# Retention and a GELU MLP on one core: seven-product groups in the first layer of blocks 3 to 6

## The chip, the cores and the metric

One core of a Trainium2 chip runs the whole program. The metric is the device time of one launch in microseconds (us). The engines are named as in the profile: PE is TensorE's matmul (PEld its weight load), DVE VectorE, ACT ScalarE, POOL GpSimd, SP SyncE, which here only issues transfers. Each engine works through its own instructions in order; a wait of one instruction holds up everything behind it on that engine.

## The reference

```python
# q, k, v: (8, 8, 576, 64) float32; w_in (512, 2048), w_out (2048, 512)
scores = matmul(q, k.T) / sqrt(64)
gamma = 1.0 - 2.0 ** (-5.0 - arange(8))                  # one decay for each head
Dmat = where(i >= j, gamma[:, None, None] ** (i - j), 0) # for positions i, j
x = matmul(scores * Dmat, v)                             # attention without softmax
x = x.transpose(0, 2, 1, 3).reshape(8 * 576, 512)        # 4608 tokens
h = x @ w_in
g = 0.5 * h * (1 + tanh(sqrt(2 / pi) * (h + 0.044715 * h ** 3)))
out = g @ w_out                                          # (4608, 512) float32
```

## The kernel before, in words

**Blocks.** The 4608 tokens are worked in nine blocks of 512 (`t` = 0 to 8, `NTB` = 9). Block `t` below 8 holds the first 512 positions of batch `t`; block 8 holds the last 64 positions of all eight batches (the tails, attended in pairs of batches: `TP`). While TensorE does the two MLP layers of block `t`, the attention of batch `t + 1` is done in between, the casts and transposes of batch `t + 2`, and the loads after that.

**A block has 30 steps.** Steps 0 to 15 are layer one, steps 16 to 29 layer two. `at(t, u, f)` hangs a piece of work behind step `u` of block `t`; `run` issues it there. So the order on each engine is written out by hand. Layer one (`up`, L474) takes the 16 column blocks of `w_in` one by one: four matmuls of 512 columns into a bank of PSUM ("a four" below), and a GELU on ScalarE into `gT`. Layer two (`prod`, L648) is done in all blocks by seven products in place of eight (Strassen and Winograd's form): VectorE makes sums of quarters of the activations (`act_sums`, L634: s1, s2, the difference in place, then s4), sums of quarters of `w_out` are made once (`weight_sums`, L623), and VectorE and ScalarE put the products together (`after`, L672), in the buffers k1, k2, k3.

**Seven products in layer one.** Blocks 7 and 8 (`WIN`) do three of four column groups of layer one in the same way. A group is 256 columns of the lower and 256 of the upper half of `w_in`, that is four column blocks. `in_sums` (L518) makes its sums of weights (during layer two of block 6), `x_sums` (L535) four sums of quarters of `xT` at the end of the block before. `up_prod` (L554) does one product: four matmuls of 256 columns. Products 1, 6, 7 and 4 of a group add up in one bank, B, so between them that bank is copied out: by ScalarE behind product 1 (into s) and behind 6 (into v), by VectorE behind 7 (into u). VectorE adds banks A and C to these copies, and ScalarE's GELU reads the results. A token such as "06" of the order `W_ORDER` means group 0, product 6; an empty one is a four.

**Attention.** For each batch four chunks of 128 positions: `score` (L379) and `masks` (L389, VectorE), `past` and `av` (L436, L455), `state` (L402) and on VectorE `scan` (L416: vs and ws, a running state with decay), which `spread` (L430) casts on ScalarE to a block-diagonal tile for `past`; `put` (L466) copies the result into `xT` on ScalarE. `later(b, c)` is scan and spread of a chunk.

**PSUM** has eight banks, handed out in the order in which they were given back (`bank`, `drop`). A bank is written again only when its last reader is done.

**Loads.** `seq` lists the loads of 256 KB in order; each takes one of sixteen buffers of the tag "ld" and gives it back when it is cast (`pump`, L141). A hold stops the list until `resume` at step 29. GpSimd casts keys and queries of batch `b` from step 16 of block `b - 2`, ScalarE the values. A copy of one element (`gate`, L978) lets GpSimd start its casts only when the last activation sum of the block has been made. All loads, the transposes (`turn_dma`, L305) and the outputs are issued on SP in one order.

## Time and profile before

| | |
|---|---|
| runs | 293.66 us median of 3 (293.11 to 294.78) |
| span of the profiled execution | 291.2 us |
| block 3, from its first matmul of layer one | 114.48 to 144.93 us |
| block 4 | 144.93 to 175.38 us |
| block 5 | 175.38 to 205.15 us |
| block 6 | 205.15 to 235.35 us |
| block 7 | 235.35 to 261.32 us |
| share of TensorE in the chain that ended last | 81% |
| loads of 256 KB, issue to landing, median | 5.2 to 5.9 us |

In the profile's lines a tile is written as output<-inputs, the number behind "x" counts instructions, and what stands in square brackets is how long the engine was idle before the instruction, and who released it. The windows give, for a stretch of time, its length and then the busy time of each engine in it.

### The profile page before, as it was taken

What the parts mean: (1) busy time and instruction counts of PE and PEld (TensorE: products, weight loads), DVE (VectorE), ACT (ScalarE), POOL (GpSimd) and SP (SyncE); (2) the same over time, 40 slices, a digit from 0 to 9 for tenths busy, and PEclk for the clock granted to TensorE, in tenths of its full rate; (3) what the DMA queues carried; (4) which work ended last, traced back from release to release, by engine and by line L of the source; (5) the groups of instructions that cost most, each with busy time, mean ns of one, the idle gap of its engine ahead of it and who ended that gap; (6) DMA issues with size and microseconds to landing.
All of it is one profiled execution on the core that took longest, in us unless ns stands there. A gap on an engine that the chain in (4) does not pass through costs nothing.

```text
span 291.2 us, 7390 instructions
## 1 busy us (share of the span) xinstructions
PE 280.6 (96%) x3028; PEld 208.4 (72%) x3028; DVE 204.2 (70%) x409; ACT 169.2 (58%) x320; POOL 100.5 (35%) x129
## 2 busy tenths in 40 slices
PE   6989998999999999999999999999999999999993
PEld 2568886888874687468845884488548887887783
DVE  5797998656864875477548834774489968974863
ACT  5278755896249545965396547664666258507810
POOL 4588869910760085008500740058030000000000
PEclk9999999999999999999999999999999999999999
DMA  7999999999989999999898979999951030003013
GB/s 196 308 367 360 379 294 240 245 235 179 224 168 243 227 204 194 254 229 199 169 234 204 229 155 239 224 202 157 265 106 38 2 144 3 0 24 122 3 36 108
DMA packets 139585, 53.95 MB, mean 185 GB/s; under 512 B 118048, under 2 KB 131360, under 8 KB 139552
## 3 DMA queue, kind: packets, MB, share of 16 engines
q1 hardware_dynamic: 138960, 52.97, 81.4%
q8 instruction: 23, 0.38, 0.5%
q10 hardware_dynamic: 592, 0.52, 0.5%
q14 instruction: 10, 0.08, 0.1%
HBM read 36.70 MB, written 9.44 MB: 158 GB/s over the span
## 4 chain that ended last, share of the span: by engine, by line
PE 81%; DMA 6%; POOL 5%; SPq 4%; DVE 1%; ACT 1%; issue 1%; POOLq 0%
PE hp L480 26%; PE opB L665 13%; PE opA L665 10%; PE opC L665 8%; PE hp L501 5%; DMA ld<-in_moe_w_in_dram 4%; PE hB L574 3%; SPq L96 3%; PE xs L459 3%; PE st L383 3%; POOL w_out_sb L771 2%; DMA ld<-in_q_dram 2%; PE hC L574 2%; PE xs L450 2%; PE opD L665 1%; PE us L408 1%
## 5 line engine op out<-in xcount | busy, mean ns | idle before, releaser
L480 PE MATMUL hp<-xT,w_in_sb 128*128 128x512 f16 x352 | 79.0, 379 | 0.0
L486 ACT ACTIVATE gT<-hp 128x512 f16<-128x512 f32 x88 | 50.1, 600 | 20.7 <-PE hp L480 20.1
L480 PEld LDWEIGHTS <-w_in_sb 128*128 128x128 f16 x352 | 34.0, 98 | 38.2
L665 PEld LDWEIGHTS <-gT 128*128 128x128 f16 x576 | 54.8, 98 | 8.9 <-issue 0.8
L665 PEld LDWEIGHTS <-s 128*128 128x128 f16 x432 | 42.1, 98 | 5.0
L642 DVE TENSOR_TENSOR s<-gT 128x512 f16<-128x512 f16 x36 | 15.6, 434 | 29.8 <-ACT gT L486 23.5
L665 PE MATMUL opA<-w_out_sb,gT 128*128 128x256 f16 x288 | 36.0, 273 | 0.4 <-ACT w_out_sb L771 0.3
L392 DVE TENSOR_TENSOR ret<-st,cm 128x512 f16<-128x512 f32 x48 | 30.1, 680 | 3.6 <-PE st L383 3.6
L469 ACT CAST xT<-xs 128x512 f16<-128x512 f32 x36 | 19.2, 591 | 18.7 <-PE xs L459 15.6
L501 PE MATMUL hp<-xT,w_in_sb 128*128 128x256 f16 x256 | 29.0, 273 | 0.0
L434 ACT CAST tbd<-ws 64x256 f16<-64x256 f32 x48 | 19.3, 403 | 15.3 <-DVE ws L425 14.7
L275 POOL TENSOR_TENSOR ck<-ld,sc 128x512 f16<-128x512 f32 x24 | 25.0, 1040 | 7.7 <-DMA ld<-in_k_dram 7.7
L978 POOL COPY gate<-s 128x1 f16<-128x1 f16 x5 | 0.9, 188 | 76.5 <-DVE s L646 76.5
L275 POOL TENSOR_TENSOR cq<-ld,sc 128x512 f16<-128x512 f32 x24 | 26.2, 1090 | 2.1 <-DMA ld<-in_q_dram 1.8
L501 PEld LDWEIGHTS <-w_in_sb 128*128 128x128 f16 x256 | 24.6, 98 | 3.1
L665 PE MATMUL opB<-wt,gT 128*128 128x256 f16 x224 | 26.8, 273 | 0.0
L262 ACT CAST cv<-ld 128x512 f16<-128x512 f32 x23 | 13.7, 618 | 18.9 <-DMA ld<-in_v_dram 18.8
L508 ACT ACTIVATE gT<-hp 128x512 f16<-128x512 f32 x32 | 18.3, 602 | 3.2 <-PE hp L501 3.0
L679 DVE TENSOR_TENSOR k<-k,opB 128x512 f32<-128x512 f32 x17 | 11.6, 685 | 12.0 <-PE opB L665 11.0
L425 DVE TENSOR_TENSOR ws<-vs,gt 128x256 f32<-128x256 f32 x24 | 18.2, 760 | 1.1
L665 PE MATMUL opB<-wt,s 128*128 128x256 f16 x144 | 17.4, 273 | 0.0
L665 PE MATMUL opC<-wt,s 128*128 128x256 f16 x144 | 17.2, 273 | 0.0
(122 smaller groups left out, 409.1 us busy)
## 6 DMA issues: line engine op xcount, KB each, us to landing
ld<-in_q_dram SPq DMA_DIRECT2D x32, 256.0 KB, 5.3
ld<-in_k_dram SPq DMA_DIRECT2D x32, 256.0 KB, 5.2
ld<-in_v_dram SPq DMA_DIRECT2D x32, 256.0 KB, 5.5
out_dram<-ost SPq DMA_DIRECT2D x16, 512.0 KB, 3.8
ld<-in_moe_w_in_dram SPq DMA_DIRECT2D x16, 256.0 KB, 5.9
ld<-in_moe_w_out_dram SPq DMA_DIRECT2D x16, 256.0 KB, 5.8
lt<-in_k_dram SPq DMA_DIRECT2D x8, 128.0 KB, 4.7
lt<-in_q_dram SPq DMA_DIRECT2D x8, 128.0 KB, 4.3
```

Source lines behind the costliest of these rows:

```text
L275: eng.tensor_tensor(out=dst.rearrange("p (h d) -> p h d", d=D), in0=raw.rearrange("p (h d) -> p h d", d=D), in1=sc[:, s0].unsqueeze(2).to_ ...
L392: nc.vector.tensor_tensor(out=r.rearrange("p (n i) -> p n i", i=128), in0=t.rearrange("p (n i) -> p n i", i=128), in1=(cm if b < PAIR else ...
L425: nc.vector.tensor_tensor(out=w, in0=uc, in1=gt, op=ALU.mult)
L434: cp(out=(tbd[b % 2][r, c, :, r] if c < NC - 1 else tbt[b % NT4][r, :, r]), in_=w[r])
L469: nc.scalar.copy(out=xT[:, g0 : g0 + 2], in_=xs.rearrange("p (n g t) -> p g n t", n=HP, g=2))
L480: nc.tensor.matmul(hp.rearrange("p (g t) -> p g t", t=TL), w_in_sb[:, ct, 128 * fc : 128 * fc + 128], xT[:, o : o + TB // TL, ct, :], star ...
L486: nc.scalar.activation(out=gT[t][:, fc].rearrange("p i n -> p (i n)"), in_=hp, func=AF.Gelu_apprx_tanh)
L501: nc.tensor.matmul(hps[n][:, 256 * x : 256 * x + 256].rearrange("p (g t) -> p g t", t=TL), w_in_sb[:, ct, 128 * (fs[n] + x) : 128 * (fs[n] ...
L508: nc.scalar.activation(out=gT[t][:, f : f + 2, 2 * u : 2 * u + 2, :].rearrange("p f i n -> p f (i n)"), in_=hp.rearrange("p (f n) -> p f n ...
L574: nc.tensor.matmul(pb[:, 256 * i : 256 * i + 256].rearrange("p (g t) -> p g t", t=TL), w(kt, i), x(kt), start=(new and i == kt == 0), stop ...
L642: nc.vector.tensor_tensor(out=s["1"], in0=a21, in1=a22, op=ALU.add)
L665: nc.tensor.matmul(op[tag][:, HD * u : HD * u + HD], lhs(f), rhs[:, f], start=(new and f == 0), stop=(f == NH - 1), skip_group_check=True,)
```

## The change

In blocks 3 to 6 (`MID`) two of the four column groups of layer one are done as seven products each, in a hand-written order (`M_ORDER`); the other eight column blocks stay fours. The sums of weights of groups 0 and 1 are made in layer two of block 2 in place of block 6, the x sums now also at the end of blocks 2 to 5. In these blocks the fourth activation sum (s4) is made by GpSimd. The scores of the next batch come at step 12 (before 9 or 11), its outputs at step 17 (15), the second pair of scores at 17 (15) and their masks at 19 and 21 (17 and 19). Scan and spread of chunks 0 and 1 of the batch after it come at steps 26 and 27 of the block before (steps 0 and 1). The cast of a tail's values moves from step 3 to 13. The sixteen load buffers become two rings of eight, "ld" and "lm"; the loads of batch 4 and later use "ld" only, since "lm" then holds sums and work buffers. The work buffers of group 0 are k1, k2 and k3 of layer two. In blocks 7 and 8 the groups' work buffers change likewise.

```diff
-    LD = 16
+    LD = 8
+    FIRST = 3
...
     def lds():
-        return sb.tile([128, 512], F32, tag="ld", name="ld", bufs=LD)
+        t = sb.tile([128, 512], F32, tag=q_ld["tag"], name="ld", bufs=LD)
+        ring[id(t)] = q_ld["tag"]
+        return t
+
+    def kept(name, shape, dt, tag="lm"):
+        return sb.tile(shape, dt, tag=tag, name=name, bufs=LD)
...
             if s[0] != "t":
-                if q_ld["free"] == 0:
+                tag = "ld" if s[0] == "b" and s[1] >= FIRST + 1 else ("ld", "lm")[q_ld["n"] % 2]
+                if q_ld["free"][tag] == 0:
                     return
-                q_ld["free"] -= 1
+                q_ld["free"][tag] -= 1
+                q_ld["n"] += 1
+                q_ld["tag"] = tag
...
     WIN = {t: 3 for t in (NTB - 2, NTB - 1)}
+    MID = {t: 2 for t in range(FIRST, NTB - 2)}
...
-        s, v, u3 = wk["s", j % 2], wk["v", j % 3], wk["u", j % 3]
+        def work(s):
+            n = j % (2 if s == "s" else 3)
+            if n == 0 and m == {"s": 1, "v": 6, "u": 7}[s]:
+                wk[s, 0] = sb.tile([128, 512], F32, tag=KT[s], name=KT[s], bufs=1)
+            return wk[s, n] if (s, n) in wk else None
+
+        s, v, u3 = work("s"), work("v"), work("u")
...
-    def act_sums(t, f0, f1, us=slice(0, 2), parts=(0, 1)):
+    def act_sums(t, f0, f1, us=slice(0, 2), parts=(0, 2, 1), eng=nc.vector):
...
+        for n in parts:
+            for o, x, y, f in (
+                ((s["1"], a21, a22, ALU.add), (s["2"], s["1"], a11, ALU.subtract)),
+                ((s["4"], a12, s["2"], ALU.subtract),), ((a21, a11, a21, ALU.subtract),),
+            )[n]:
+                eng.tensor_tensor(out=o, in0=x, in1=y, op=f)
...
+    M_ORDER = "01 02 05 11 06 12  15 07 16  04 17 03  c0 14  13   c2  c1 e0  c3 e2 e1 d0 d2 d1 d3 e3".split(" ")
     for n in range(GW):
-        at(NTB - 3, 17 + 2 * n, lambda n=n: in_sums(n, (3, 2)))
-        at(NTB - 3, 18 + 2 * n, lambda n=n: in_sums(n, (4, 1)))
-    at(NTB - 3, 27, lambda: x_sums(NTB - 2))
+        t, u = (FIRST - 1, 17 + 2 * n) if n < 2 else (NTB - 3, 19)
+        at(t, u, lambda n=n: in_sums(n, (3, 2)))
+        at(t, u + 1, lambda n=n: in_sums(n, (4, 1)))
+    for t in (*MID, NTB - 2):
+        at(t - 1, 27, lambda t=t: x_sums(t))
...
-        at(t, 3, lambda b=b: tail_values(b))
+        at(t, 13 if t in MID else 3, lambda b=b: tail_values(b))
...
-        s0, o0, s1, o1 = U2 if t == 1 else (11 if t in (2, 3) else 9, 15, 15, 24)
+        s0, o0, s1, o1 = U2 if t == 1 else (12, 17, 17, 24) if t in MID else (11 if t == 2 else 9, 15, 15, 24)
...
-            at(t, 17, lambda b=b: masks(b, 2))
-            at(t, 19, lambda b=b: masks(b, 3))
+            at(t, s1 + 2, lambda b=b: masks(b, 2))
+            at(t, s1 + 4, lambda b=b: masks(b, 3))
...
-                at(t + 1, c, lambda c=c, nb=b + 1: later(nb, c))
+                at(*((t, 26 + c) if t + 1 in MID else (t + 1, c)), lambda c=c, nb=b + 1: later(nb, c))
...
+                    elif w[0] in "cde":
+                        n = "ced".index(w[0])
+                        act_sums(t, 2 * int(w[1]), 2 * int(w[1]) + 2, parts=(n,), eng=P if n == 1 else V)
```

In `M_ORDER` "c" makes s1 and s2 of a quarter of the column blocks, "d" the difference in place (both on VectorE), "e" makes s4 (on GpSimd).

More of the change, by code (lines that the diff above doesn't have):

```diff
@@ L68, in drop @@
         spare.append(home.pop(id(t))[0])
+    ring = {}
     def lds():
-        return sb.tile([128, 512], F32, tag="ld", name="ld", bufs=LD)
+        t = sb.tile([128, 512], F32, tag=q_ld["tag"], name="ld", bufs=LD)
[3 more added lines that the diff above has]
+        return sb.tile(shape, dt, tag=tag, name=name, bufs=LD)
     def ldt():
@@ L138, with pump @@
             seq.append(("h",))
-    q_ld = {"next": 0, "free": LD, "hold": False}
-    def pump(freed=0):
-        q_ld["free"] += freed
+    q_ld = {"next": 0, "n": 0, "tag": None, "free": {"ld": LD, "lm": LD}, "hold": False}
+    def pump(raw=None):
+        if raw is not None:
+            q_ld["free"][ring.pop(id(raw))] += 1
         while q_ld["next"] < len(seq) and not q_ld["hold"]:
@@ L257, in cast @@
         a = att[b]
-        raw = a["raw"].pop((key, c))
+        a["gone"] = raw = a["raw"].pop((key, c))
         dst = a[key][:, 512 * c : 512 * c + 512]
@@ L518, in in_sums @@
     def in_sums(j, ns):
-        if not wi:
-            for g in range(0, GW, 2):
-                for n in "234":
-                    wi[n, g // 2] = sb.tile([128, 2, 512], F16, tag="ld", name="wi" + n, bufs=LD)
+        for n in "234":
+            if (n, j // 2) not in wi:
+                wi[n, j // 2] = kept("wi" + n, [128, 2, 512], F16, "lm" if j < 2 else "ld")
         c, lo, hi = slice(256 * (j % 2), 256 * (j % 2) + 256), slice(256 * j, 256 * j + 256), slice(DF // 2 + 256 * j, DF // 2 + 256 * j + 256)
@@ L537, in x_sums @@
             for n in ("12", "34"):
-                x = sb.tile([128, 2, 4, 2, TL], F16, tag="ld", name="x" + n, bufs=LD)
+                x = kept("x" + n, [128, 2, 4, 2, TL], F16)
                 xw[int(n[0])], xw[int(n[1])] = x[:, 0], x[:, 1]
-            for n in range(3):
-                for s in "svu" if n < 2 else "vu":
-                    wk[s, n] = sb.tile([128, 512], F32, tag="ld", name="w" + s, bufs=LD)
+            for s in "svu":
+                wk[s, 1] = kept("w" + s, [128, 512], F32)
+        if t == NTB - 2:
+            for s in "vu":
+                wk[s, 2] = kept("w" + s, [128, 512], F32, "ld")
         o = 8 * (t % 2) if t < B else GM
@@ L552 @@
     wk, wb, due = {}, {}, []
+    KT = {"s": "k1", "v": "k2", "u": "k3"}
     def up_prod(t, j, m):
@@ L640, in act_sums @@
         s = {n: x[:, lo, us] for n, x in gs[t].items()}
-        if 0 in parts:
-            nc.vector.tensor_tensor(out=s["1"], in0=a21, in1=a22, op=ALU.add)
-            nc.vector.tensor_tensor(out=s["2"], in0=s["1"], in1=a11, op=ALU.subtract)
-            nc.vector.tensor_tensor(out=a21, in0=a11, in1=a21, op=ALU.subtract)
-        if 1 in parts:
-            nc.vector.tensor_tensor(out=s["4"], in0=a12, in1=s["2"], op=ALU.subtract)
+        for n in parts:
[4 more added lines that the diff above has]
+                eng.tensor_tensor(out=o, in0=x, in1=y, op=f)
     def prod(t, m, u, fs=range(NH)):
@@ L771, in cast_w @@
         eng(out=dst, in_=src)
-        pump(1)
+        pump(src)
     HALF = (2, 6)
@@ L778, in cc @@
         cast(b, key, c, eng)
-        pump(1)
+        pump(att[b].pop("gone"))
     V, P, A = nc.vector, nc.gpsimd, nc.scalar
@@ L1007 @@
                     steps.append(half)
-            todo = deque(f + h for f in range(2 * WIN.get(t, 0), NH) for h in (0, NH))
-            for w in (W_ORDER if t in WIN else ()):
+            todo = deque(f + h for f in range(2 * {**WIN, **MID}.get(t, 0), NH) for h in (0, NH))
+            for w in (W_ORDER if t in WIN else M_ORDER if t in MID else ()):
                 def mixed(w=w):
@@ L1023, in token @@
                     elif w[0] in "ab":
-                        act_sums(t, 2 * int(w[1]), 2 * int(w[1]) + 2, parts=("ab".index(w[0]),))
+                        act_sums(t, 2 * int(w[1]), 2 * int(w[1]) + 2, parts=((0, 2), (1,))["ab".index(w[0])])
+                    elif w[0] in "cde":
+                        n = "ced".index(w[0])
+                        act_sums(t, 2 * int(w[1]), 2 * int(w[1]) + 2, parts=(n,), eng=P if n == 1 else V)
                     else:
                         up_prod(t, int(w[0]), int(w[1]))
-                steps.append((mixed, 0 if w[:1] in ("a", "b", "Q") else 1 if w else 2))
-            for f in range(0 if t == 1 or t in WIN else NH):
+                steps.append((mixed, 0 if w[:1] in ("a", "b", "c", "d", "e", "Q") else 1 if w else 2))
+            for f in range(0 if t == 1 or t in WIN or t in MID else NH):
                 steps.append(lambda f=f: up(t, f))
```

## The prediction

> **What bounds the kernel now.** I read the busy shares first, then the table of windows, the chain that ended last, and the timeline of VectorE and ScalarE where a block ends.

> ```profile
> PE 280.6 (96%) x3028; PEld 208.4 (72%) x3028; DVE 204.2 (70%) x409; ACT 169.2 (58%) x320; POOL 100.5 (35%) x129
> ```
> ```profile
> core 0: us, PE busy (x) PEld busy (x) DVE busy (x) ACT busy (x) POOL busy (x), PEclk, DMA share, GB/s
> ...
> 144.93:159.60 14.67, 14.67 (x91) 6.88 (x90) 9.93 (x22) 11.11 (x22) 0.96 (x1) 1.00 1.01 218
> 159.60:175.38 15.78, 15.78 (x222) 14.08 (x220) 9.04 (x16) 8.07 (x16) 8.63 (x9) 1.00 1.06 191
> ```
> The two windows are the two layers of block 4. TensorE is busy in every microsecond of both, at full clock (1.00), so time there falls only if its work falls, and any wait of TensorE that the change makes is added whole. VectorE is 19.0 of 30.45 us busy, the DMA engines all the time.

> The chain gives the rate of each form:
> ```profile
> 144.93 8.63 PE hp L480 x40
> ...
> 235.35 0.44 PE hB L574 x4
> 235.78 0.44 PE hA L574 x4
> 236.22 0.44 PE hC L574 x4
> 236.66 0.87 PE hB L574 x8
> ```
> A 512-column matmul costs 8.63/40 = 0.216 us, a 256-column one of a seven-product group 0.87/8 = 0.109. The last four lines are the start of block 7, which has such groups already: products 1, 2, 5 of group 0, then 1 of group 1 and 6 of group 0, without a gap.

> How block 6 hands over to block 7, on VectorE and then ScalarE:
> ```profile
> 231.88 0.42 DVE L422 TENSOR_TENSOR vs<-us,ws 128x256 f32<-128x256 f32 x1
> 232.34 0.42 DVE L425 TENSOR_TENSOR ws<-vs,gt 128x256 f32<-128x256 f32 x1
> 233.64 0.69 DVE L679 TENSOR_TENSOR ost<-k,opB 128x512 f32<-128x512 f32 x1 [0.88 <-PE opB L665]
> 234.24 0.42 DVE L550 TENSOR_TENSOR x<-xT 128x512 f16<-128x512 f16 x1
> ...
> 235.38 0.42 DVE L550 TENSOR_TENSOR x<-xT,x 128x512 f16<-128x512 f16 x1
> 235.71 0.68 DVE L679 TENSOR_TENSOR ost<-k,opC 128x512 f32<-128x512 f32 x1
> ```
> ```profile
> 206.73 0.82 ACT L434 CAST tbd<-ws 64x256 f16<-64x256 f32 x2
> ...
> 235.88 0.58 ACT L594 COPY ws<-hB 128x512 f32<-128x512 f32 x1 [2.27 <-PE hB L574]
> ```
> The addition behind product 4 starts 1.71 us before the block's end (235.35), the four x sums end at +0.36. ScalarE is idle (2.27) and copies the bank of product 1 at +0.53; product 6 adds to that same bank, so it may start only after this copy.

> **The change, part by part**, in blocks 3 to 6.

> (a) *TensorE work.* A group of four column blocks was 16 matmuls of 0.216 = 3.45 us and becomes 28 of 0.109 = 3.05. Saved: 0.41 for each of 2 x 4 groups, **-3.26 us**. Nothing else of TensorE's work changes; the moved scores and outputs are the same matmuls.

> (b) *A wait at the start of each of the four blocks.* The x sums now end blocks 2 to 5 too, and the scan and spread of chunks 0 and 1 (L425, L434) move from the new block's first steps to the end of the old one. On VectorE that puts, behind the addition of product 4: four x sums, then vs and ws of chunk 1. From -1.71: 2.07 to the end of the x sums (233.64 to 235.71), 0.88 for vs and ws (231.88 to 232.76): chunk 1 is ready at +1.24. On ScalarE its spread (0.82, two casts) stands ahead of the copy of product 1's bank: 1.27 to 2.09, copy 0.58, done at 2.70. Product 6 is TensorE's fifth step, due at 4 x 0.435 = 1.74. It waits 0.96, and TensorE being in order, all of layer one behind it waits with it. The next copies (bank of product 6 before product 7, and so on) are 0.4 us ahead in block 7 and keep their distance. **4 x 0.96 = +3.84 us.** So the wait alone takes back more than (a).

> (c) *VectorE in the middle of the block.* Added per block: four operations of 0.69 for each of two groups = 5.5 us and the x sums 1.7; removed: four sums of 0.45 = 1.8. That is 19.0 + 5.4 = 24.4 of about 30.5 (block 4). What matters is where it is late. From the block's start, with 0.96 from (b): scores of the next batch at 14 x 0.435 + 6 x 0.863 + 0.96 = 12.2; four masks 2.47 (154.00 to 156.40) from 12.5 to 15.0; three pairs of activation sums at 0.80 (149.93 to 150.73) to 17.4; four differences at 0.34 to 18.8; vs and ws to 19.7; the addition behind product 6 to 20.4. That addition reads the bank to which product 7 adds. TensorE comes to product 7 after scores 0.55, two fours 1.73, product 1 1.75, outputs and scores 1.6 (189.85 to 191.44), products 6 and 5 3.5: 21.3. VectorE has 0.9 us to spare; with a tail batch (blocks 3, 4, 6), two more masks (1.2) against 0.65 more of TensorE, 0.35.

> But GpSimd now makes the fourth sums in this very stretch, and then its casts. Its price for an f16 sum is not in the trace; the nearest row, its f16 from f32 product L275, is 1.04. What the two engines do to each other is:
> ```profile
> 213.29 1.24 POOL L275 TENSOR_TENSOR e<-lt,sc 128x512 f16<-128x512 f32 x1 [10.54 <-DMA lt<-in_k_dram]
> 213.56 1.26 DVE L644 TENSOR_TENSOR gT<-gT 128x512 f16<-128x512 f16 x1
> ```
> A VectorE difference of 0.42 takes 1.26 beside a GpSimd operation: 0.84 more. Lower bound nothing; upper bound three sums and two casts at 0.84 = 4.2, less the spare time: 3.3 (block 5), 3.85 (others), 14.9 in all. The row L425, which runs beside the casts in much of its calls, has 0.76 mean against 0.42 alone: 0.34 more. I take three meetings at 0.34 = 1.0: hidden in block 5, 0.65 in the three others, **+1.95 us**.

> (d) *Weight sums of two groups in block 2 instead of block 6.* Eight operations of 0.42. In block 6 GpSimd is idle (no busy time from 219.80 on); in block 2 it casts keys and queries from 101.67 to 111.85. VectorE's list from 101.6 to the addition of product 4 is 9.9 us with them, 11.2 are there: 1.3 to spare. Bounds: 0, and 8 x 0.84 - 1.3 = 5.4. At 0.34 each: 2.7 - 1.3, **+1.4 us**. Block 6 loses eight such operations, behind a busy TensorE: nothing.

> (e) *x sums and ws beside the casts* that GpSimd still makes at the end of blocks 2, 3 and 5 (113.54 and 143.85 now). Bounds 0 and two meetings of 0.84 at four block ends, 6.7; I take 0.34 at three: **+1.0 us**.

> (f) *Half the load ring.* From batch 4 on eight buffers serve twelve loads, so loads 9 to 12 on SP wait for the first four casts, and those now stand behind GpSimd's sums: up to 3.1 us later. Behind them on SP stand the tail loads, the transposes, the output and the next loads. The ninth load is now issued at 102.51, 132.89, 162.54, 187.64, about when the casts begin (101.67, 132.07, 162.11, 192.34), and the scores that need the transposes come at step 12 instead of 9 or 11. Cost 0; upper bound 1.1 per block where the last value load delays the ScalarE copies into xT behind it (in block 3 they end 0.7 before the block does): 3.3.

> Scalar work rises by two copies of 0.58 a group, 2.3 us in layer one on 11.1 of 14.67: covered, were it not for (b). The k1 to k3 buffers that the groups now share are read last before they are wanted.

> Sum: -3.26 + 3.84 + 1.95 + 1.4 + 1.0 = **+4.9 us**. The profiled execution's span, 291.2, becomes 296.1. It lies 2.46 under the median of the runs, 293.66; with the same distance the time is **298.6 us**.

> **Rivals.** *Only the wait (b) is real*, and the meetings of VectorE and GpSimd fall into spare time: 293.66 - 3.26 + 3.84 = 294.2. For it: VectorE keeps 6 us idle per block. Against: its idle time is not where the sums stand.

> *The saving is kept, 290.4.* This is the other side: ScalarE would have to finish the spread of chunk 1 by about +1.1, so that product 6 finds its bank copied at 1.74. That happens if the x sums and the scan together take under 2.0 instead of 2.95, or run ahead of product 4's addition. For it: in block 7 the same five products run without a gap. Against: block 7 has no spread in front of the copy, and the order on both engines is fixed.

> *VectorE becomes the bound.* Each GpSimd operation holds up a VectorE one in full: (c) goes to 14.9, and 293.66 - 3.26 + 3.84 + 14.9 = 309, less where one wait covers another, about 306 to 309. [...] Against the full price: by the same rows most ws fall into a gap (0.76 mean, not 1.26).

> *The loads set the period.* SP is busy from 121.62 to 151.84 without a pause, 30.2 us for a block. If the ring adds 1.5 in each of blocks 3 to 5: 294.2 + 4.5 = 298.7, with TensorE waiting on xT.

> **Chances.** Forecast 0.60; only the wait 0.15; saving kept 0.08; VectorE the bound 0.10; loads 0.07. The time is that of the forecast, 298.6. The range goes from just under the bare wait, 293.9, to 305.0, where half of the upper bounds of (c) and (d) are paid; outside are the saving, a little of the first rival and most of the third, two tenths. A measurement here can tell about 0.5% (292.2 to 295.1) from no change: faster 0.08, same 0.13 (the first rival but for its slower edge), slower 0.79.

> **What would show it.** TensorE gaps of about 1 us before product 6 in blocks 3 to 6, ended by ScalarE's copy of product 1's bank; longer ones before product 7 of layer two, ended by VectorE's k2 addition; layer one of those blocks at 13.6 plus the gap; VectorE sums of over 0.8 us beside GpSimd. The prediction is wrong if product 6 starts by +1.8, or if the largest gaps stand before scores or at xT, which would be the loads.

## The result, and the profile after

| | before | after |
|---|---|---|
| median of the runs | 293.38 us (4 runs, 292.65 to 294.78) | 319.74 us (4 runs, 318.49 to 320.82) |
| ratio | | **1.0893** (95%: 1.0856 to 1.0930), slower |
| span of the profiled execution | 291.2 us | 318.3 us |

The forecast was 298.6 us with a range up to 305.0. The direction was right, the size was not: 26.4 us were added to the median, 4.9 were forecast. Slow runs are left out of all comparisons: there was one, of the kernel before with s4 on GpSimd, 414.71 us at a mean clock of 0.66.

The page of the changed kernel: busy time of each engine, the granted clock of TensorE in 40 slices, and the shares of the chain that ended last.

```profile
PE 284.9 (90%) x3124; PEld 219.5 (69%) x3124; DVE 241.3 (76%) x441; ACT 175.6 (55%) x336; POOL 121.8 (38%) x145
...
PEclk9999999999999899999999999999899899999999
...
PE 53%; DVE 22%; DMA 7%; POOL 6%; ACT 4%; SPq 3%; issue 3%; DVEq 0%; POOLq 0%; ACTq 0%
```

TensorE was 96% busy and is 90% busy; its share of the chain fell from 81% to 53%, and VectorE has 22% of it. Three slices of the clock show an 8, so the clock fell somewhere inside them.

The windows of the changed kernel, block 3 to block 6, each from its first matmul of layer one. Columns: length, then the busy time of TensorE, its weight load, VectorE, ScalarE and GpSimd, granted clock, DMA share, GB/s.

```profile
119.49:153.70 34.21, 30.30 (x334) 23.21 (x332) 26.73 (x45) 18.86 (x37) 14.67 (x14) 1.00 0.81 160
153.70:189.78 36.08, 30.31 (x334) 23.21 (x332) 28.80 (x49) 21.72 (x44) 14.98 (x15) 1.00 0.81 167
189.78:222.87 33.09, 29.63 (x310) 22.50 (x308) 25.44 (x43) 17.79 (x35) 14.57 (x14) 1.00 0.87 167
222.87:262.30 39.43, 33.24 (x319) 24.44 (x316) 30.30 (x52) 19.06 (x39) 8.43 (x8) 0.91 0.39 88
```

These blocks took 30.45, 30.46, 29.76 and 30.20 us before. (The block starts given with the profile before were read off the chain that ended last; the first matmuls of layer one start 0.17 earlier, at 114.31, 144.76, 175.22, 204.98 and 235.18 for blocks 3 to 7. The lengths are nearly the same.) In the first three TensorE is idle for 3.91, 5.77 and 3.46 us. Block 6 is idle for 6.19 us, and there the matmuls themselves take longer: 33.24 us of work at a mean clock of 0.91.

What TensorE waited for in the changed kernel (total us, times, longest):

```profile
PE opB L686 <- DVE k L700: 11.4, 5, 3.3
PE hB L589 <- ACT k L615: 7.6, 4, 2.8
PE opB L686 <- DVE s L667: 3.4, 4, 1.0
```

The first line is product 7 of layer two waiting for the k2 addition, in blocks 2 to 6. The second is product 6 of layer one waiting for ScalarE's copy of product 1's bank, in blocks 3 to 6. The third is product 6 of layer two waiting for the sums s2. In what follows a wait is measured from one matmul's start to the next, less their usual distance, which gives a little more than the view:

| wait of TensorE, us | block 2 | 3 | 4 | 5 | 6 | sum |
|---|---|---|---|---|---|---|
| product 6 of layer one (ScalarE's copy) | | 1.16 | 2.97 | 1.17 | 3.00 | 8.30 |
| product 6 of layer two (s2) | | 1.15 | 1.15 | 0.63 | 1.15 | 4.08 |
| product 7 of layer two (k2 addition) | 3.42 | 2.07 | 2.07 | 2.07 | 2.53 | 12.16 |

Together 24.5 us. Shorter waits add 0.9 (0.3 before), the half clock some 4.9 (last section), and 3.26 were saved: 24.5 + 0.6 + 4.9 - 3.26 = 26.8, beside the 27.1 by which the spans differ.

### The profile page after: what moved, and what is told of

It is laid out like the page before. It is cut to its first block, busy times and chain, and to the rows that moved or that the text cites. A ratio compares the mean times of both kernels' runs of the same rounds, so it can differ in the third digit from the quotient of the medians.

```text
span 318.3 us, 7688 instructions
## 1 busy us (share of the span) xinstructions
PE 284.9 (90%) x3124; PEld 219.5 (69%) x3124; DVE 241.3 (76%) x441; ACT 175.6 (55%) x336; POOL 121.8 (38%) x145
## 4 chain that ended last, share of the span: by engine, by line
PE 53%; DVE 22%; DMA 7%; POOL 6%; ACT 4%; SPq 3%; issue 3%; DVEq 0%; POOLq 0%; ACTq 0%
PE hp L492 12%; PE opB L686 9%; PE hB L589 7%; DVE s L667 6%; PE opA L686 5%; DVE ret L404 4%; PE hp L513 4%; DMA ld<-in_moe_w_in_dram 4%; DVE gT L667 3%; PE hC L589 3%; PE opC L686 3%; SPq L104 3%; DVE x L564 3%; POOL w_out_sb L792 2%; DMA ld<-in_v_dram 2%
## 5 line engine op out<-in xcount | busy, mean ns | idle before, releaser
L686 PEld LDWEIGHTS <-gT 128*128 128x128 f16 x576 | 56.8, 101 | 23.3 <-issue 13.2
L492 PE MATMUL hp<-xT,w_in_sb 128*128 128x512 f16 x224 | 54.5, 382 | 0.0
L667 POOL TENSOR_TENSOR s<-gT,s 128x512 f16<-128x512 f16 x16 | 19.1, 1193 | 78.1 <-DVE s L667 61.0
L686 PE MATMUL opB<-wt,gT 128*128 128x256 f16 x224 | 29.8, 292 | 11.4 <-DVE k L700 11.4
L492 PEld LDWEIGHTS <-w_in_sb 128*128 128x128 f16 x224 | 21.6, 98 | 19.7 <-issue 0.3
L498 ACT ACTIVATE gT<-hp 128x512 f16<-128x512 f32 x56 | 32.4, 599 | 4.8 <-PE hp L492 4.6
L481 ACT CAST xT<-xs 128x512 f16<-128x512 f32 x36 | 19.2, 590 | 18.8 <-PE xs L471 15.6
L287 POOL TENSOR_TENSOR cq<-ld,sc 128x512 f16<-128x512 f32 x24 | 26.8, 1119 | 1.4 <-DMA ld<-in_q_dram 1.0
L513 PEld LDWEIGHTS <-w_in_sb 128*128 128x128 f16 x256 | 24.4, 98 | 4.0 <-POOL w_in_sb L792 0.9
L589 PEld LDWEIGHTS <-wi 128*128 128x128 f16 x168 | 16.7, 100 | 13.7 <-issue 8.7
L589 PEld LDWEIGHTS <-w_in_sb 128*128 128x128 f16 x224 | 22.1, 99 | 5.5 <-issue 0.6
L667 DVE TENSOR_TENSOR s<-s,gT 128x512 f16<-128x512 f16 x36 | 22.8, 635 | 1.5
L589 PE MATMUL hB<-x,wi 128*128 128x256 f16 x112 | 16.5, 281 | 7.8 <-ACT k L615 7.6
L667 DVE TENSOR_TENSOR gT<-gT 128x512 f16<-128x512 f16 x36 | 23.3, 673 | 0.0
```

The lines of the kernel that those rows point to most:

```text
L287: eng.tensor_tensor(out=dst.rearrange("p (h d) -> p h d", d=D), in0=raw.rearrange("p (h d) -> p h d", d=D), in1=sc[:, s0].unsqueeze(2).to_ ...
L481: nc.scalar.copy(out=xT[:, g0 : g0 + 2], in_=xs.rearrange("p (n g t) -> p g n t", n=HP, g=2))
L492: nc.tensor.matmul(hp.rearrange("p (g t) -> p g t", t=TL), w_in_sb[:, ct, 128 * fc : 128 * fc + 128], xT[:, o : o + TB // TL, ct, :], star ...
L498: nc.scalar.activation(out=gT[t][:, fc].rearrange("p i n -> p (i n)"), in_=hp, func=AF.Gelu_apprx_tanh)
L513: nc.tensor.matmul(hps[n][:, 256 * x : 256 * x + 256].rearrange("p (g t) -> p g t", t=TL), w_in_sb[:, ct, 128 * (fs[n] + x) : 128 * (fs[n] ...
L589: nc.tensor.matmul(pb[:, 256 * i : 256 * i + 256].rearrange("p (g t) -> p g t", t=TL), w(kt, i), x(kt), start=(new and i == kt == 0), stop ...
```

## The experiments

Each is compared with the kernel before, run on the same chip. "From after" or "from before" says which kernel was edited.

### The fourth activation sum: on GpSimd or on VectorE

*From after:* s4 back on VectorE.

```diff
-                        act_sums(t, 2 * int(w[1]), 2 * int(w[1]) + 2, parts=(n,), eng=P if n == 1 else V)
+                        act_sums(t, 2 * int(w[1]), 2 * int(w[1]) + 2, parts=(n,))
```

> The changed kernel with one thing undone: the fourth activation sums of blocks 3 to 6 are made on VectorE again. [...] Rival W (VectorE simply has too much work in these blocks): 1.4 us more of it per block, so 319 to 325 us.

Theory P, here and in the expectations below, is that the sums on GpSimd stretch VectorE's sums and differences beside them (the prediction's row has 1.26 for 0.42) and push the casts back. It had 305 to 310 us here.

Measured: 309.48 us, ratio 1.0557 (1.0509 to 1.0605), 10.3 us less than the changed kernel although VectorE has sixteen more instructions. The waits for s2 are gone (4.08), those before product 7 in blocks 3 to 6 are 4.72 in place of 8.74 (2 to 4 were expected to be left of both), and one stretch at half clock is left of three.

VectorE in block 4 of the changed kernel (start, duration, operation):

```profile
172.32 0.42 DVE L667 TENSOR_TENSOR s<-gT 128x512 f16<-128x512 f16 x1
...
173.11 0.42 DVE L667 TENSOR_TENSOR s<-gT 128x512 f16<-128x512 f16 x1
173.56 1.26 DVE L667 TENSOR_TENSOR s<-s,gT 128x512 f16<-128x512 f16 x1
174.75 0.41 DVE L667 TENSOR_TENSOR s<-gT 128x512 f16<-128x512 f16 x1
175.19 1.26 DVE L667 TENSOR_TENSOR s<-s,gT 128x512 f16<-128x512 f16 x1
176.38 3.22 DVE L667 TENSOR_TENSOR gT<-gT 128x512 f16<-128x512 f16 x4
...
179.97 0.81 DVE L437 TENSOR_TENSOR ws<-vs,gt 128x256 f32<-128x256 f32 x1
180.70 0.67 DVE L700 TENSOR_TENSOR k<-k,opB 128x512 f32<-128x512 f32 x1
```

GpSimd in the same stretch:

```profile
173.34 1.21 POOL L667 TENSOR_TENSOR s<-gT,s 128x512 f16<-128x512 f16 x1 [4.24 <-DVE s L667]
174.97 1.20 POOL L667 TENSOR_TENSOR s<-gT,s 128x512 f16<-128x512 f16 x1 [0.43 <-DVE s L667]
176.59 1.20 POOL L667 TENSOR_TENSOR s<-gT,s 128x512 f16<-128x512 f16 x1 [0.42 <-DVE s L667]
178.08 1.24 POOL L287 TENSOR_TENSOR ck<-ld,sc 128x512 f16<-128x512 f32 x1
```

The two engines alternate. An s4 starts when its s2 is done, and the s2 of the next pair, started 0.2 us later, ends only behind the end of that s4 (174.82 and 174.55): 1.26 for 0.42. The next s4 waits for it. So a pair takes 1.63 us (173.34 to 174.97). The four differences then meet the last s4 and the first cast and take 3.22. The k2 addition ends at 181.37, and product 7 starts at 181.43.

VectorE in the same place with s4 on VectorE:

```profile
174.03 1.42 DVE L667 TENSOR_TENSOR gT<-gT 128x512 f16<-128x512 f16 x4
...
176.16 1.22 DVE L437 TENSOR_TENSOR ws<-vs,gt 128x256 f32<-128x256 f32 x1
177.31 0.67 DVE L700 TENSOR_TENSOR k<-k,opB 128x512 f32<-128x512 f32 x1
```

The differences take 1.42. From the last tail mask to the end of the addition it is 7.3 us here (170.64 to 177.98) and 9.05 there (172.32 to 181.37), with four more sums here.

*From before:* the same sums on GpSimd, in a kernel whose VectorE has room.

```diff
-            nc.vector.tensor_tensor(out=s["4"], in0=a12, in1=s["2"], op=ALU.subtract)
+            e4.tensor_tensor(out=s["4"], in0=a12, in1=s["2"], op=ALU.subtract)
...
+                        return lambda: act_sums(t, f - 1, f + 1, e4=P if t in (3, 4, 5, 6) else V)
```

> The kernel before with one part of the change alone: the fourth activation sums of blocks 3 to 6 on GpSimd. Theory P: each GpSimd sum takes 1.2 us and VectorE operations beside it up to 1.26, but VectorE has spare time in this kernel and the sums are spread over layer one; 293 to 297 us. Rival (the sums on GpSimd are costly by themselves, whatever else VectorE does): the 12.9 us of layer two's waits come with them, 303 to 307.

Measured: 294.42 us (median of seven runs), ratio 1.0033 (1.0002 to 1.0064). About 1 us for the same sixteen instructions. An s4 takes 1.17 to 1.21 here too, but the pairs stand apart: in block 4 the s4 of the first pair runs from 151.06 to 152.23, and VectorE's next sum starts at 152.53. So the price is not that of the instruction but of the place where it stands.

### The scan of chunk 1 ahead of the block's start

*From after:* chunk 1 (vs, ws and its spread) issued at step 26, ahead of product 4's addition and of the x sums, in place of step 27.

```diff
-                at(*((t, 26 + c) if t + 1 in MID else (t + 1, c)), lambda c=c, nb=b + 1: later(nb, c))
+                at(*((t, 26) if t + 1 in MID else (t + 1, c)), lambda c=c, nb=b + 1: later(nb, c))
```

> The changed kernel with scan and spread of chunk 1 one step earlier (26 in place of 27), ahead of the addition of product 4 and the x sums. Theory B (the spread stands in front of the copy of product 1's bank): the waits of 1.2 us before product 6 of layer one at the starts of blocks 3 and 5 vanish, those of 3.0 at blocks 4 and 6 fall to 2 or stay, where xT is late; 316 to 318 us. Rival (all four waits come from late loads or late sums): no change, 319 to 320.

Measured: 313.49 us, ratio 1.0694 (1.0653 to 1.0735), 6.3 us less than the changed kernel. Product 6 of layer one no longer waits in blocks 3 and 5; in blocks 4 and 6 it still waits 1.46 and 1.39. So the spread is worth about 1.2 to 1.6 in each block, and blocks 4 and 6 have something more.

ScalarE at the start of block 3 (119.49) in the changed kernel shows the first cause alone:

```profile
120.92 0.82 ACT L446 CAST tbd<-ws 64x256 f16<-64x256 f32 x2 [2.55 <-DVE ws L437]
121.76 0.59 ACT L615 COPY k<-hB 128x512 f32<-128x512 f32 x1
```

The spread runs from +1.43 to +2.25, the copy ends at +2.86, and product 6 starts at 122.40 (+2.91). The prediction had +1.27, +2.09 and +2.70.

VectorE at the start of block 4 (153.70) shows another:

```profile
152.16 0.69 DVE L700 TENSOR_TENSOR ost<-k,opB 128x512 f32<-128x512 f32 x1 [1.94 <-PE opB L686]
153.18 0.95 DVE L564 TENSOR_TENSOR x<-xT 128x512 f16<-128x512 f16 x1 [0.33 <-ACT xT L481]
154.16 1.28 DVE L564 TENSOR_TENSOR x<-x,xT 128x512 f16<-128x512 f16 x1
```

The x sums wait 0.33 for ScalarE's last copy into xT, and two of them meet GpSimd's casts of the tail (at 152.81 and 154.12): 2.86 from the first to the scan, against 1.47 in block 5, where no cast runs. That is 1.4 + 0.4 = 1.8 us, which is what block 4 waits more than block 5 (2.97 against 1.17). Both are there in the kernel before too: the tail's casts start 0.91 before block 4 (143.85, the block at 144.76; here 0.89), and the last copy into xT ends 0.54 before it (here 0.55). Only no x sums run there to meet them. At the start of block 6 (222.87) VectorE has the same picture (0.95 and 1.21, an idle 0.44 for xT), but for another reason, which the load ring shows below.

### The weight sums of groups 0 and 1 earlier in block 2

*From after:* the three read-only sums at steps 4 and 6 of block 2, the one in place at 17 and 18.

```diff
+        if n < 2:
+            at(t, 4 + 2 * n, lambda n=n: in_sums(n, (3, 2, 4)))
+            at(t, 17 + n, lambda n=n: in_sums(n, (1,)))
+            continue
```

> The changed kernel with the read-only sums of weights of groups 0 and 1 at steps 4 and 6 of block 2, where GpSimd is idle, and only the two sums in place left at steps 17 and 18. Theory P: the wait of 3.4 us before product 7 of block 2 falls under 1, and the stretch of half-speed matmuls behind it (16 in 3.39 us) goes; 314 to 316 us. Rival (the wait there is VectorE's sum of work): the same operations are in the block, 319 to 320.

Measured: 316.83 us, ratio 1.0808 (1.0768 to 1.0847), 2.9 us less than the changed kernel. The wait before product 7 in block 2 falls from 3.42 to 1.79; under 1 and 314 to 316 us were expected. The two sums in place still stand in front of the k2 addition, at 1.26 and 1.06. The other waits together rise by 0.7, and one stretch at half clock is there in place of three, so that most of the 2.9 is likely the clock's.

VectorE in block 2 of the changed kernel:

```profile
103.19 1.26 DVE L543 TENSOR_TENSOR wi<-w_in_sb 128x512 f16<-128x512 f16 x1
104.48 1.15 DVE L543 TENSOR_TENSOR wi<-wi,w_in_sb 128x512 f16<-128x512 f16 x1
...
106.75 1.06 DVE L543 TENSOR_TENSOR wi<-w_in_sb,wi 128x512 f16<-128x512 f16 x1
107.74 1.26 DVE L543 TENSOR_TENSOR w_in_sb<-w_in_sb 128x512 f16<-128x512 f16 x1
108.92 0.67 DVE L700 TENSOR_TENSOR k<-k,opB 128x512 f32<-128x512 f32 x1
```

Four sums take 4.73 us in place of 1.68, all beside GpSimd's casts, and all four stand in front of the k2 addition, which TensorE needed at 106.2.

### The three together

*From after:* the three edits above at once.

> The changed kernel with the three edits of the runs before together (fourth sums on VectorE, scan and spread of chunk 1 at step 26, read-only sums of weights early in block 2). If the causes are separate, their gains add: 319.7 - 10.3 - 6.2 - 2.9 = 300.3, so 299 to 302 us; what is left are the waits on k2 before product 7 (about 1.5 each), the late xT at blocks 4 and 6 and half-clock stretches only where a wait stays over 2.5. Rival (one late queue behind all of them, so that a wait removed comes back at the next place): 304 to 308.

Measured: 299.87 us, ratio 1.0231 (1.0176 to 1.0287). 19.9 of the 26.4 us are gone, 0.5 us from the sum of the three. No stretch at half clock is left. The waits that remain are five before product 7 (1.85, 1.51, 1.51, 0.99, 0.71) and two in layer one (1.08, 1.20), 8.85 in all.

### The load ring alone

*From before:* two rings of eight buffers, the loads of batch 4 and later in one of them.

```diff
-    LD = 16
+    LD = 8
...
+                tag = "ld" if s[0] == "b" and s[1] >= 4 else ("ld", "lm")[q_ld["n"] % 2]
+                if q_ld["free"][tag] == 0:
```

> The kernel before with one part of the change alone: the load buffers as two rings of eight, loads from batch 4 on in one of them. Theory (the ring costs only where the casts that free it start late): the casts start at 16.8 us of a block as before, the ninth load loses under 1 us; 293 to 295 us. Rival (half the ring is itself the cause of the late xT): 296 to 300 us, with waits at xT in blocks 4 to 6.

Measured: 293.22 us, ratio 0.9999 (0.9964 to 1.0034). The ring alone costs nothing, though it shifts work: in block 5 the first cast of the tail starts 2.7 before block 6 (204.44, the block at 207.12) where it was 4.5 before it (200.53 and 204.98). Nothing stands behind it there that is wanted at once. With s4 on GpSimd as well, still from before:

> The kernel before with two parts of the change, half the ring and the fourth sums of blocks 3 to 6 on GpSimd, without the seven products in layer one. Theory: the last of these sums delays the casts by about 1.5 us and, through the ring, the last loads by as much, which layer two still hides; 294 to 297 us. Rival (these two make the late xT by themselves): over 298 us.

Measured: 294.33 us, ratio 1.0067 (1.0035 to 1.0098); the s4 alone gave 1.0033 (1.0002 to 1.0064), so that the ring's share, if any, is within the intervals.

In the changed kernel the x sums stand behind it. SP in block 5, issues with their start and time:

```profile
200.88 1.33 SPq L109 DMA_DIRECT2D ld<-in_q_dram  x1
212.43 0.37 SPq L109 DMA_DIRECT2D ld<-in_v_dram  x1
...
215.31 1.79 SPq L94 DMA_DIRECT2D lt<-in_k_dram  x2
```

The first line is the eighth load. Behind it SP stands still for 10.2 us, until GpSimd, whose casts wait for the last s4, has made its first cast (211.17 to 212.41). The tail's loads behind (L94) start at 215.31, so that its two casts (222.07 and 223.31) start 0.8 before block 6 in place of 4.5, in the middle of the x sums. The same stall in block 3 (129.56 to 143.26) changes nothing at block 4, where these casts were as late before.

It is the place of the last s4 that makes the casts late, not its engine. With s4 on VectorE (the first experiment) GpSimd's first cast in block 5 starts 20.97 behind the block's first matmul, against 21.39 here and 17.12 in the kernel before; the tail's casts start 0.96 before block 6, and product 6 of layer one still waits 2.90 there.

### The queues put in order again

*From the kernel with the three edits:* in blocks 3 to 5 GpSimd's first three casts go ahead of its wait for the last s4, so that the loads go on; in blocks 2 to 6 the scan of chunk 2 goes behind the k2 addition; the weight sums in place go to steps 21 and 22 of block 2.

```diff
-            at(t, 17 + n, lambda n=n: in_sums(n, (1,)))
+            at(t, 21 + n, lambda n=n: in_sums(n, (1,)))
...
-        at(t, o0 + 1, lambda b=b: later(b, 2))
+        at(t, 20 if t in MID or t == 2 else o0 + 1, lambda b=b: later(b, 2))
...
+        first = t0 in MID
+        if first:
+            ut = [13, 13, 17, 14] + ut[4:]
...
-            at(t0, ut[0], lambda t=t0: nc.gpsimd.tensor_copy(out=gate, in_=gs[t]["4"][:, NH - 1, 1, 0:1]))
+            at(t0, 16 if first else ut[0], lambda t=t0: nc.gpsimd.tensor_copy(out=gate, in_=gs[t]["4"][:, NH - 1, 1, 0:1]))
```

> As the run with three edits, and two queues reordered: the first two key casts and the first query cast of blocks 3 to 5 stand on GpSimd at steps 13 and 14, beside VectorE's masks and ahead of the gate, so that the ring's ninth to twelfth loads can start earlier; and the scan of chunk 2 stands at step 20, behind k2's addition. Theory: xT comes in time (waits before product 6 of blocks 4 and 6 under 0.5) and product 7 waits under 0.5; 294 to 297 us. Rival (VectorE has too much work for these blocks in any order): waits stay, 299 to 302.

Measured: 293.91 us, ratio 1.0031 (1.0007 to 1.0055). Windows of blocks 4 and 5 of this kernel, columns as above:

```profile
145.94:176.31 30.37, 30.03 (x335) 23.39 (x333) 25.91 (x52) 20.28 (x41) 8.99 (x10) 1.00 1.04 196
176.31:205.28 28.97, 28.97 (x310) 22.63 (x308) 24.15 (x49) 19.44 (x38) 10.74 (x11) 1.00 1.07 217
```

Block 5 has no wait at all: 28.97 against 29.76 before, the whole saving of two groups (0.81). Blocks 2 to 4 and 6 take 30.19, 30.80, 30.37 and 31.09 (before 29.76, 30.45, 30.46 and 30.20), and give it back in small waits. Those named by the view of waits:

```profile
PE xs L462 <- ACT tbd L446: 1.8, 3, 1.2
PE hB L589 <- ACT k L621: 0.8, 2, 0.6
```

The first is the outputs waiting for a spread whose scan was moved back, the second product 7 of layer one waiting for the copy behind product 6.

Two kernels tried to mend that. One makes group 2's weight sums early in block 6 too and puts the scan of chunk 2 back to step 18 there:

> As the run with the queues reordered, with two places of block 6 mended: the scan of chunk 2 goes back to step 18 there, since GpSimd casts nothing in that block, and the read-only sums of group 2's weights go to step 8. Theory (TensorE's work is 3.26 us less, and what is left of the gain is lost only at named waits, 1.3 of 2.6 us in block 6): 291.8 to 292.8 us against 293.1. Rival (the reordered kernel's lag is spread over many small gaps): no change, 293.5 to 294.2.

Measured: 294.40 us, ratio 1.0039 (1.0015 to 1.0063). The wait of 1.28 late in block 6 becomes 0.59; one of 1.17 comes up earlier in that block, and 0.73, 0.61 and 0.54 in others. The other moves only the scan back:

> As the run with the queues reordered, with the scan of chunk 2 back at step 18 in block 6 alone (its wait there was 1.3 us); the sums of group 2's weights stay at steps 19 and 20, since their early place at step 8 met the tail casts of GpSimd and made a new wait of 1.2. Theory (the loss is a sum of named waits): 1 us less than the run with the queues reordered, 292.4 to 293.3, and so no measurable difference to the kernel before. Rival (VectorE in block 6 is full and the wait moves on): 293.7 to 294.4.

Measured: 294.57 us, ratio 1.0031 (1.0003 to 1.0059). Its wait in block 6 is 0.60 in place of 1.28, and at the start of block 3 there are two new ones, 1.30 and 1.33. Both lie above what was expected of them; why the waits come up elsewhere was not followed. The three kernels can't be told apart, and none beats the kernel before.

*From the reordered kernel:* s4 on GpSimd again, and nothing else.

```diff
-                        act_sums(t, 2 * int(w[1]), 2 * int(w[1]) + 2, parts=(n,))
+                        act_sums(t, 2 * int(w[1]), 2 * int(w[1]) + 2, parts=(n,), eng=P if n == 1 else V)
```

> As the run with the queues reordered, with one thing put back: the fourth sums of blocks 3 to 6 on GpSimd. [...] Rival (only the queue order mattered, and moving work off VectorE is as good as keeping it there): 293 to 295.

Measured: 304.13 us, ratio 1.0359 (1.0311 to 1.0407); theory P had 299 to 304. The ratios differ by 0.0328, which is 9.6 us; the spans by 10.1 (302.5 and 292.4). TensorE's clock is full throughout, so these are waits alone: 4.13 for s2, 4.41 before product 7, some 3.1 at the outputs (a spread that is late), 1.90 before product 6 of layer one. Block 4's VectorE has the same two lines as the changed kernel:

```profile
167.55 1.26 DVE L667 TENSOR_TENSOR s<-s,gT 128x512 f16<-128x512 f16 x1
168.73 3.22 DVE L667 TENSOR_TENSOR gT<-gT 128x512 f16<-128x512 f16 x4
```

### Waits of chosen lengths

*From before:* 4, 5, 7, 8 and 10 fillings of a scratch tile on VectorE in front of the k2 addition of blocks 2 to 6, so that TensorE waits before product 7 and nothing else is changed.

```diff
+            for _ in range({2: 4, 3: 5, 4: 7, 5: 8, 6: 10}.get(t, 0)):
+                nc.vector.memset(pause, 0.0)
```

> The kernel before, with VectorE held back ahead of k2's addition by 4, 5, 7, 8 and 10 fills of a scratch tile (about 0.48 us each) in blocks 2 to 6, so that TensorE waits before product 7 by about 0.9, 1.5, 2.4, 2.9 and 3.8 us; nothing else is changed. Theory C (TensorE's clock falls to a half for some 3 us behind a wait of over about 2.5 us): 16 matmuls in 1.75 us behind the three shorter waits, in about 3.4 behind the two longer ones. Rival (the slow stretches of the changed kernel come from something else than the wait): 1.75 behind all. About 306 us.

Measured: 315.74 us (one run, so no interval; 293.33 before). The waits are 1.35, 1.96, 2.87, 3.98 and 5.50 us, 15.7 in all, of 22.4 added. Behind the first two TensorE goes on at full clock; behind the other three matmuls take twice as long for a time, 1.5, 2.6 and 2.1 us more. These five alone would also fit the expectation, a limit of about 2.5 us on the length of a wait (the shortest with half clock behind it in the changed kernel is 2.53); the waits of the changed kernel do not, and the last section takes this up.

## Why the prediction was right and wrong

| step of the prediction | forecast, us | measured, us |
|---|---|---|
| (a) TensorE's work | -3.26 | -0.79 for one block (0.81 forecast) |
| (b) spread of chunk 1 ahead of the copy | +3.84 | 1.16 and 1.17 in blocks 3 and 5, where it is alone: 4.66 for four |
| (c) VectorE in mid-block, meeting GpSimd | +1.95 | 4.08 + 8.74 = 12.8 |
| (d) weight sums in block 2 | +1.4 | 3.42 |
| (e) x sums beside casts | +1.0 | 1.81 (block 4, over 1.16) |
| (f) half the load ring | 0 | 1.83 (block 6, over 1.17) |
| half clock behind long waits | none | 4.9 |

**(a) was right.** Block 5 of the reordered kernel shows it whole.

**(b) was right in mechanism, and 0.2 us too small a block.** The copy of product 1's bank holds up product 6, as named; undoing it alone takes the wait out of blocks 3 and 5. Nearly all of the 0.2 is the block's start. The prediction took 235.35 for block 7, from the chain, and product 6 as due 1.74 behind that; TensorE's timeline of the kernel before has

```profile
235.18 0.60 PE L574 MATMUL hB<-xT,w_in_sb 128*128 128x256 f16 x4
...
236.93 0.60 PE L574 MATMUL hB<-x,wi 128*128 128x256 f16 x4
```

so product 6 was due at 236.93. From 235.18 the same sum gives a spread at +1.44, the end of the copy at +2.87 and a wait of 1.13.

**(c) is the step that failed.** Its mechanism held, and its price was mis-sized. The prediction counted three meetings at 0.34, from the mean of ws (L425), and gave 4.2 a block as the upper bound. What the timeline of block 4 shows is two s2 at 1.26 (0.84 more each), four differences at 3.22 (1.80 more than in the kernel with s4 on VectorE) and a ws at 0.81 (0.39 more): 3.87, nearly the bound. The mean of L425 was the wrong row. By that mean most of its calls miss the casts, while in a row without gaps an s4 is started by the s2 just ahead of the operation that it blocks: in block 4 three of the four meet a sum or the differences. The right row was on record beside it, the difference of 1.26. The s2 of block 4 have the same price, 1.26 for 0.42 behind an s4 of 1.20. The rival "VectorE becomes the bound" had this price (14.9) and was given 0.10; its 309 us still lay 11 below the measured time, since (d) to (f) and the clock come on top. The reordered kernel with s4 on GpSimd gives the price free of the clock: 9.6 to 10.1 us, from a move that takes sixteen instructions off VectorE. In the kernel before, where VectorE is idle behind its sums, the same move costs 1. Of the 12.8, 4.7 stay with s4 on VectorE, where a ws of 1.22 beside a cast stands in front of the addition in block 4; they are gone in the reordered kernel, where the scan stands behind the addition and three casts stand earlier.

**(d) had the wrong deadline.** The prediction gave the eight sums the time up to the addition behind product 4, with 1.3 us to spare. But four of them stand in front of the k2 addition behind product 6. In the kernel before that addition ends at 105.18; here TensorE asks for it at 106.2, and the block began 0.27 later, so 0.8 were to spare. The four sums take 4.73, a pair of masks stands among them, and the addition ends at 109.59. In the reordered kernel, where the sums in place stand behind the addition (and the scan too), block 2 has no such wait.

**(e) was right in place, too small in price.** At block 4 the two casts cost 1.4, not 0.34, and xT 0.4, which the prediction could have had from its own numbers (the copies end 0.7 before the block, product 4's addition some 1.0 before it). At block 3 no cast met the x sums.

**(f) was taken at nothing, and costs 1.8 in block 6.** The prediction set the ninth load of each block beside the begin of the casts, and in its list block 5 stands out: 187.64 and 192.34, so that a load that waits for the casts comes 4.7 us later, where the other three lose under 0.9. It passed over that one. The last s4 stands later in the block than before, on either engine, and the casts behind it: the load is issued at 212.43, and the tail's casts, 3.7 us later against the block's end, meet the x sums. That it is the late casts is borne out by the reordered kernel: with the first three casts ahead of the sums, the tail's casts of block 5 stand at 201.13, 4.2 before block 6, and product 6 doesn't wait there. (That kernel has two other edits too. The wait was 1.20 in the kernel with the three edits, where the casts were still late.) The ring was not undone alone in the changed kernel, so that its own share there is argued from the order of the issues, not measured.

**The half clock was not in the prediction at all.** In the changed kernel it stands behind waits of 2.53 us and more; the largest wait that the forecast had at one place was 1.4.

Of what the prediction said would show it: the gaps before product 6 and before product 7 stood where named, ended by ScalarE's copy and the k2 addition, and VectorE's sums beside GpSimd took over 0.8. None of the largest stood before scores, and xT has 0.4 us of those in blocks 4 and 6.

## What to carry to other kernels

Work moved from a busy VectorE to GpSimd is to be priced at the row where the two engines meet, not at a mean over calls that mostly miss each other; a dependent pair split over the two (s2, then s4) met here at each step where the pairs followed each other without a gap, at 1.26 for 0.42. Each added instruction is checked against the first deadline behind it on its queue, not against the room in the whole stretch. A shift that costs nothing by itself (the ring) can cost as soon as another edit puts something behind it that can't wait.

## What the runs showed of the hardware

```profile
105.81:109.23 3.42, 0.58 (x6) 0.38 (x4) 3.42 (x5) 0.70 (x2) 3.30 (x4) 1.00 0.88 195
109.23:112.64 3.41, 2.99 (x15) 2.12 (x15) 3.38 (x6) 0.62 (x1) 1.77 (x2) 0.51 1.27 209
112.64:116.05 3.41, 3.41 (x60) 3.04 (x59) 3.20 (x7) 1.07 (x2) 2.23 (x2) 0.99 1.33 209
...
211.63:215.04 3.41, 1.50 (x14) 1.20 (x13) 3.38 (x6) 1.10 (x3) 3.41 (x4) 1.00 0.43 97
215.04:218.45 3.41, 3.41 (x61) 3.08 (x59) 3.38 (x7) 0.94 (x2) 3.41 (x4) 1.00 1.33 234
...
225.28:228.69 3.41, 1.08 (x9) 0.87 (x9) 2.07 (x5) 1.70 (x4) 0.00 (x0) 1.00 1.06 203
228.69:232.11 3.42, 3.42 (x15) 1.98 (x14) 0.88 (x2) 2.40 (x5) 0.00 (x0) 0.51 1.01 334
...
249.17:252.59 3.42, 1.05 (x11) 0.80 (x9) 3.38 (x6) 0.67 (x2) 1.63 (x2) 1.00 0.16 33
252.59:256.00 3.41, 3.41 (x17) 2.42 (x17) 3.32 (x8) 0.14 (x1) 0.00 (x0) 0.51 0.24 44
```

The windows here in which TensorE was idle for 2.33 to 2.84 us were followed by one at half clock; the one idle for 1.91 was not. The wait of 2.97 (155.34 to 158.42) falls across an edge at 157.01, 1.56 before and 1.41 behind it, and costs no clock. The three half-clock windows hold 9.8 us of matmul time, half of which, 4.9, is lost.

The kernel with chosen waits has its grid elsewhere (its edges lie 2.84 us further on), and shows what followed a longer wait:

```profile
204.23:207.64 3.41, 1.18 (x11) 0.90 (x10) 2.54 (x6) 1.72 (x4) 3.41 (x4) 1.00 0.70 157
207.64:211.05 3.41, 1.82 (x9) 1.28 (x9) 2.55 (x5) 0.00 (x0) 3.41 (x4) 0.52 0.52 101
211.05:214.46 3.41, 3.41 (x19) 2.36 (x17) 1.59 (x3) 0.00 (x0) 0.14 (x1) 0.50 1.12 209
214.46:217.88 3.42, 3.42 (x60) 3.07 (x58) 0.54 (x2) 2.00 (x5) 0.00 (x0) 0.98 0.41 80
```

A window at half clock with TensorE busy for 1.82 us was followed by another at half clock (0.50); the next, busy throughout, by one at 0.98. In the five profiles that have such stretches (the changed kernel, three from it, and this one) eleven windows between block 2 and the last product, idle for some 2.2 to 3.0 us, are each followed by one at half clock, and no window there idle for 1.91 or less is, unless the clock was half already. So in the changed kernel a wait of 2.5 to 3.4 us costs 1.5 to 1.7 us more or nothing, by where it falls on the grid.

None of these windows was idle throughout: 2.33 of 3.41 us were enough in the changed kernel, and 2.23 in the one with chosen waits. What sets the grid, and what follows a window idle for 1.91 to 2.2 us, no run shows.
